# Sigmoid attention feeding a SiLU feed-forward: the x of one quad on two engines, one more gated pair of casts, all SBUF products on GpSimd, and a re-timed order

## The chip, the cores and the metric

The kernel runs on one core of a Trainium2 chip. Its time is the device time of one execution in microseconds, and a kernel is described by the median of several executions. The trace comes from one profiled execution; it records what each engine did and when: TensorE (PE, its weight loads PEld), VectorE (DVE), ScalarE (ACT), GpSimd (POOL), and the DMA queues issued from SyncE (SP), GpSimd and ScalarE.

## The reference

```python
# q, k, v: (8 batches, 12 heads, 448 positions, 64)
scores = (q @ k.T) / sqrt(64) - log(448)
attn = 1 / (1 + exp(-scores))          # a sigmoid, not a softmax
x = (attn @ v)                         # to 3584 tokens x 768
h = x @ w_in                           # w_in 768 x 2048
g = h * (1 / (1 + exp(-h)))
out = g @ w_out                        # w_out 2048 x 768, float32
```

## The kernel before

**Tiling.** Attention works on *quads*: four heads of one batch, so a batch has three quads and quad i belongs to batch i // 3. A quad's 448 keys are taken in seven *score steps* of 64 (`score_step`, line 172: four 64x64 matmuls into one pair of PSUM banks), each followed by a sigmoid on ScalarE (line 178) into `attnT`. When a quad's seven sigmoids are there, 28 matmuls multiply by v (`value_steps`, line 188), and `to_x` scales the sum into x, transposed, in half precision. `to_x` has three forms: two VectorE instructions when the sum lies in the two `ffp` banks (line 201), one VectorE instruction over both banks (line 206), or, with `shared`, one bank by VectorE (line 203) and the other by ScalarE (line 204).

PSUM has four pairs of banks: `att0`, `att1`, `att2` and the two `ffp` banks, which are called pair 3.

**Products by seven instead of eight.** From batch 1 on, both matrix products of the feed-forward are done blockwise with seven block products in place of eight, with sums of blocks as operands. `x_sums` (line 218) makes the sums of x, `w_in_sums` (317 to 319) and `w_in_last_sum` (323) those of w_in, `w_sum` (432, in two halves) those of w_out, `g_sums` (454 to 460) those of the gated hidden rows. `ff1(b, ...)` computes x times w_in for batch b: 14 groups of twelve L350 matmuls; ScalarE copies partial results to SBUF (381), VectorE combines them (385), ScalarE takes the sigmoid (369), and the product by the value follows. For six of eight results per batch that product reads SBUF only, and the table `GP` says for each whether GpSimd (371) or VectorE (373) does it; the other two read PSUM and are VectorE's. `ff2(n, rows, ...)` multiplies one or two blocks of 128 tokens by w_out (L473, eight matmuls per product); between its products VectorE copies (484), combines (487) and scales (506, 545) PSUM, and the stores go out from SP.

**The order.** Every engine runs its instructions in the order in which they are written, so the source decides the order; nothing is planned at run time.

- The opening is the list `INIT`: "s" is the next score step and its sigmoid, ("T", kind, quad, pair) transposes k (1) or q (0) of a quad with TensorE and copies it out with VectorE (158), ("V", quad, pair, r) a value step, "X" a `to_x`, "L" a load, "W" a quarter of w_in, "F" a number of steps of batch 0's first product `ff1_first`, "D" dummy matmuls that read a tile of zeros.
- `PROGRAM` then runs batch 0's first product (96 matmuls on line 282) and stops at the named steps for a "v", a visit of batch 1's attention (`visit`: up to two units, each a score step or the value steps of a quad with its x), or for one of the sums ("w", "l", "x", "y", "1", "2"; "f" writes a product that was put off, line 300). The last visit holds quad 5's value steps and its x.
- In stage b, from 1 to 7, `ff1(b)` runs, and then `ff2` on the blocks that are ready; `PHASES[b - 1]` says after how many L473 matmuls a visit of batch b+1's attention comes and how many units it takes.

**Loads of later quads.** k and q of quads 6 and on are loaded in float32 to `st32` by SP (`fetch`, 123), cast by GpSimd to `st16` (`cast`, 126), and transposed by a DMA from SP (`dma_transpose`, 140); v is loaded from GpSimd's queue (119). For each later quad j, `fetch(j)` is written after the visit with score step 0 of quad j-2, and `prepare(j)`, its two casts and two transposes, after the visit with score step 3 of that quad; for the first quad of the pair that a stage begins with, `prepare` stands at the start of the stage instead, behind two one-element memsets of `st16` on VectorE (738). A cast must wait for the memset of its tile, which runs in VectorE's order: that holds GpSimd's casts back until VectorE has come to that place.

Of the kernel before, what the change touches and what calls it, by code (L numbers as in the profile page):

```python
# [16 lines left out]
def kernel(  # L17
# [9 lines left out]
    nc = tc.nc  # L27

    B, H, S, D = q.shape
# [5 lines left out]
    NQ = H // 4  # L35
# [16 lines left out]
    def sb(name, shape, dtype=F16):  # L52
        return pool.tile(shape, dtype, tag=name, name=name)
# [15 lines left out]
    st16 = [sb(f"st16_{t}", [P, R, 2, D]) for t in range(2)]  # L69
# [126 lines left out]
    def to_x(i, pair, shared=False):  # L196
        b, n = divmod(i, NQ)
        x = xT[min(b, 1)].rearrange("p (j n) s -> p n j s", n=NQ)[:, n]
        if pair == 3:
            for j in range(2):  # L200
                nc.vector.tensor_scalar_mul(x[:, j], ffp[j][:, :S], SX)
        elif shared:
            nc.vector.tensor_scalar_mul(x[:, 0], att[pair][:, 0, :S], SX)
            nc.scalar.activation(x[:, 1], att[pair][:, 1, :S], AF.Copy, scale=SX)
        else:
            nc.vector.tensor_scalar_mul(x, att[pair][:, :, :S], SX)  # L206
# [4 lines left out]
    def x_sums(cs, lo=0, hi=4):  # L211
        x = xT[1]
        b11, b12 = x[:, cs, SH:], x[:, cs, :SH]
        ch = slice(cs.start + KC, cs.stop + KC)
        b21, b22 = x[:, ch, SH:], x[:, ch, :SH]
        t1, t2, t3, t4n = (xs[:, i, cs] for i in range(4))
        for o, p, q in ((t1, b12, b11), (t2, b22, t1), (t3, b22, b12), (t4n, b21, t2))[lo:hi]:
            nc.vector.tensor_sub(o, p, q)
# [4 lines left out]
    def flush():  # L223
        while later:
            later.pop(0)()

    def at(u, f):
        events.setdefault(u, []).append(f)
# [3 lines left out]
    def visit(us, n=3, hold=False):  # L232

        if not hold:
            flush()
        pairs = [p for p in used if p < n][: len(us)]
        for p in pairs:
            used.remove(p)
            used.append(p)
        for u in us:  # L240
            if u[0] == "a":
                pr = pairs.pop(0)
                value_steps(u[1], pr, range(R))
                to_x(u[1], pr)
                if u[1] >= 2 * NQ:
                    x_sums(slice(u[1] % NQ, u[1] % NQ + 1))
        for u in us:
            if u[0] == "s":
                pr = pairs.pop(0)
                score_step(u[1], u[2], pr)  # L250
                sigmoid(u[1], u[2], pr)
        for u in us:
            for f in events.pop(u, ()):
                f()
# [316 lines left out]
        load32(0, i)  # L571
        load16(2, i)

    def prepare(i):
        for t in (1, 0):
            cast(t, i)
            dma_transpose(t, i)
# [30 lines left out]
    def T(kind, i, pair):  # L608
# [3 lines left out]
            t_copy(kind, i, pair, half, dve)  # L612

    PROGRAM = (
        (8, "v", 0), (19, "v", 0), (32, "v", 0), (38, "v", 0), (43, "w", 1),
        (43, "v", 0), (50, "v", 0), (59, "w", 0), (59, "v", 0), (69, "v", 0),
        (71, "w", 3), (74, "v", 0), (86, "w", 2), (89, "v", 0), (94, "v", 0),
        (96, "l", 1), (96, "x", 0), (96, "x", 1), (96, "v", 0), (96, "x", 2),
        (96, "f", 0), (96, "l", 0), (96, "y", 2), (96, "y", 1), (96, "y", 0),
        (96, "1", 0), (96, "2", 0),  # L620
    )

    INIT = (
        ("L", 1, 3), ("D", 2), ("s",), ("s",), ("T", 1, 1, 2), ("s",), ("s",), ("s",),
        ("T", 0, 1, 3), ("L", 1, 4), ("s",), ("L", 0, 3), ("T", 1, 2, 2), ("L", 0, 4),
        ("s",), ("T", 0, 2, 3), ("s",), ("s",), ("L", 2, 1), ("L", 1, 5),
        ("T", 1, 3, 2), ("s",), ("V", 0, 2, 0), ("V", 0, 2, 1), ("V", 0, 2, 2),
        ("L", 2, 2), ("L", 0, 5), ("s",), ("W", 0), ("W", 1), ("V", 0, 2, 3),
        ("V", 0, 2, 4), ("T", 0, 3, 3), ("s",), ("V", 0, 2, 5), ("W", 2),
        ("V", 0, 2, 6), ("X", 0, 2), ("s",), ("T", 1, 4, 3), ("L", 2, 4), ("s",),  # L630
        ("s",), ("T", 0, 4, 2), ("L", 2, 5), ("V", 1, 3, 0), ("V", 1, 3, 1),
        ("L", 2, 3), ("s",), ("s",), ("T", 1, 5, 2), ("W", 3), ("s",), ("V", 1, 3, 2),
        ("T", 0, 5, 2), ("V", 1, 3, 3), ("s",), ("V", 1, 3, 4), ("V", 1, 3, 5), ("s",),
        ("s",), ("V", 2, 2, 0), ("V", 2, 2, 1), ("V", 2, 2, 2), ("V", 2, 2, 3),
        ("V", 1, 3, 6), ("s",), ("V", 2, 2, 4), ("V", 2, 2, 5), ("V", 2, 2, 6), ("s",),
        ("X", 1, 3), ("X", 2, 2, True), ("F", 4), ("F", 4),
    )

    us = units_of(1)
# [2 lines left out]
    for what, *a in INIT:  # L642
        if what == "s":
            u = scores[ns]
# [22 lines left out]
    for i in range(NQ + 1, B * NQ - 2):  # L667
        at(("s", i, 0), lambda j=i + 2: (gate(j) if j < 2 * NQ + 1 else None, fetch(j)))
        if i % NQ < NQ - 1:
            at(("s", i, 3), lambda j=i + 2: prepare(j))  # L670

# [14 lines left out]
    for n, kind, c in PROGRAM:  # L688
# [8 lines left out]


    PHASES = (
        ((19, 3), (33, 3), (46, 3), (58, 3), (67, 3), (82, 3), (89, 2), (97, 3), (107, 1)),  # L700
        ((19, 3), (33, 3), (47, 3), (53, 3), (62, 3), (76, 3), (85, 2), (91, 3), (107, 1)),
        ((19, 3), (33, 3), (48, 3), (54, 3), (63, 3), (77, 3), (85, 3), (91, 2), (99, 1)),
        ((17, 3), (32, 3), (46, 3), (53, 3), (62, 3), (76, 3), (83, 3), (92, 2), (97, 1)),
        ((14, 3), (23, 3), (37, 3), (40, 3), (47, 3), (58, 3), (62, 2), (67, 3), (75, 1)),
        ((19, 3), (32, 3), (44, 3), (50, 3), (60, 3), (75, 3), (83, 3), (91, 2), (99, 1)),
        (),
    )

    GP = (
        (1, 1, 1, 1, 1, 1), (1, 1, 1, 1, 1, 1), (1, 1, 1, 1, 0, 1), (1, 1, 1, 1, 1, 1),  # L710
        (1, 1, 1, 1, 1, 1), (1, 1, 1, 1, 1, 1), (0, 1, 1, 1, 1, 1),
    )

    ORD = (
# [15 lines left out]
    for b in range(1, B):  # L730
        parts = FF2[b - 1]
        late = (parts[0][0] + parts[0][1]) * P > b * S
        if parts[0][1] == 2 and not late:
            g_sums(parts[0][0], 4)
        if b + 1 < B:

            for t in range(2):
                nc.vector.memset(st16[t][:, 0, 0, 0:1], 0.0)  # L738
            prepare(b * NQ + NQ + 1)
        groups = ((1 - used[-1], 3), (2, used[-1])) if b == 1 else ((1, 3), (2, 0))  # L740
        used.sort()
        ff1(b, groups, GP[b - 1], ORD[b - 1])
        us = units_of(b + 1) if b + 1 < B else []

        def run():
            for i, (n, rows) in enumerate(parts):
                yield from ff2(n, rows, parts[i + 1][1] if i + 1 < len(parts) else 0, late and i == 0)

        it = run()
        done = 0  # L750
        nu = 0
        for target, m in PHASES[b - 1]:
            while done < target:
                next(it)
                done += 1
            visit(us[nu : nu + m])
            nu += m
        for _ in it:
            pass
# [30 lines left out]
```

## Time and profile before

| what | value |
|---|---|
| median of 7 runs | 374.09 us (373.25 to 375.67) |
| the profiled execution | 373.25 us |
| its span | 371.5 us |
| TensorE matmuls busy | 357.6 us (96%) |
| ScalarE busy | 255.3 us (69%) |
| VectorE busy | 229.4 us (62%) |
| GpSimd busy | 157.0 us (42%) |
| TensorE clock granted | full in all forty slices |

The span is what the trace covers; what lies around it makes up the rest of the execution's time. A line of the timeline gives the start, the time to the end of the last of its instructions, engine, line, operation, what is written and read with its size, the count, and in brackets the idle time of the engine ahead of it with what ended that. Matmuls overlap: one L473 matmul is drawn 0.33 us long while the next begins 0.163 us after it.

### The profile page before, as it was taken

How to read it: one execution, taken by the hardware profiler on the slowest of the kernel's cores; microseconds unless marked ns; L12 is line 12 of the kernel's file. 1: busy time of each engine (PE TensorE's matmuls, PEld its weight loads, DVE VectorE, ACT ScalarE, POOL GpSimd, SP SyncE). 2: the span in 40 equal slices, each digit the busy share in tenths (PEclk: the TensorE clock that was granted, in tenths of full speed). 3: DMA queues.
4: the chain of work that ended last, by engine and by line, in shares of the span. 5: the costliest groups of instructions: out<-in, count | busy, mean ns of one | idle time of the engine just before them, and what ended most of it. 6: DMA issues, size and time to landing. Idle time of an engine off the chain costs nothing. (4 is left out here: it accounts for less than half of the span.)

```text
span 371.5 us, 8711 instructions
## 1 busy us (share of the span) xinstructions
PE 357.6 (96%) x3596; PEld 239.1 (64%) x3596; DVE 229.4 (62%) x399; ACT 255.3 (69%) x290; POOL 157.0 (42%) x160
## 2 busy tenths in 40 slices
PE   8679999999999999999999999999999999999995
PEld 3344446964579655894549955598447965489663
DVE  2673689958765574586747656618367557437762
ACT  3999886777856798476874778567995779846200
POOL 8961430494305923169111782019630591004500
PEclk9999999999999999999999999999999999999999
DMA  8999999849897099563994539982699705130133
GB/s 143 191 171 205 232 224 180 155 104 165 130 237 161 6 172 211 159 150 50 193 211 118 123 52 204 205 188 48 85 180 220 164 11 116 38 86 2 42 87 86
DMA packets 64840, 51.14 MB, mean 138 GB/s; under 512 B 36896, under 2 KB 61728, under 8 KB 64800
## 3 DMA queue, kind: packets, MB, share of 16 engines
q1 hardware_dynamic: 48544, 35.24, 44.6%
q0 software_dynamic: 15328, 14.32, 25.9%
q10 hardware_dynamic: 928, 1.02, 0.8%
q8 instruction: 28, 0.46, 0.5%
q14 instruction: 12, 0.10, 0.1%
HBM read 45.61 MB, written 11.01 MB: 152 GB/s over the span
## 5 line engine op out<-in xcount | busy, mean ns | idle before, releaser
L178 ACT ACTIVATE attnT<-att,bias_s 128x896 f16<-128x896 f32 x168 | 157.3, 1008 | 28.9 <-PE att L172 28.4
L371 POOL TENSOR_TENSOR gT<-attnT,gT 128x896 f16<-128x896 f32 x40 | 75.2, 1908 | 56.2 <-ACT gT L369 56.1
L126 POOL CAST st<-st 128x896 f16<-128x896 f32 x36 | 33.8, 960 | 123.1 <-DVE st L738 54.4
L350 PEld LDWEIGHTS <-w_in_sb 128*128 128x128 f16 x672 | 64.4, 98 | 1.8 <-issue 0.9
L350 PE MATMUL att<-xT,w_in_sb 128*128 128x224 f16 x588 | 61.2, 259 | 0.4 <-DVE xT L206 0.4
L473 PEld LDWEIGHTS <-gT 128*128 128x128 f16 x416 | 39.1, 98 | 29.9 <-issue 6.5
L381 ACT COPY attnT<-att 128x896 f32<-128x896 f32 x35 | 31.7, 905 | 38.5 <-PE att L350 38.3
L473 PEld LDWEIGHTS <-gs 128*128 128x128 f16 x384 | 34.8, 98 | 32.6 <-issue 12.3
L369 ACT ACTIVATE gT<-attnT 128x896 f16<-128x896 f32 x42 | 39.9, 951 | 17.6 <-DVE attnT L385 16.3
L473 PE MATMUL ffp<-w_out_sb,gT 128*128 128x384 f16 x288 | 51.5, 326 | 0.0
L350 PEld LDWEIGHTS <-sw 128*128 128x128 f16 x504 | 48.3, 98 | 0.0
L172 PE MATMUL att<-qkT,qkT 64*64 64x448 f16 x588 | 41.9, 358 | 4.2 <-ACT attnT L178 3.4
L206 DVE TENSOR_SCALAR xT<-att 128x896 f16<-128x896 f32 x22 | 24.0, 1091 | 27.3 <-PE att L188 24.1
L385 DVE TENSOR_TENSOR attnT<-att,attnT 128x896 f32<-128x896 f32 x28 | 30.5, 1090 | 15.1 <-PE att L350 14.2
L473 PE MATMUL ffp<-wt,gs 128*128 128x384 f16 x192 | 35.9, 327 | 0.5 <-DVE snap L484 0.5
L473 PE MATMUL ffp<-w_out_sb,gs 128*128 128x384 f16 x192 | 36.1, 327 | 0.0
L350 PE MATMUL att<-xT,sw 128*128 128x224 f16 x336 | 35.0, 259 | 0.0
L484 DVE TENSOR_SCALAR snap<-ffp 128x384 f32<-128x384 f32 x40 | 22.1, 553 | 19.4 <-PE ffp L473 19.3
L188 PE MATMUL att<-attnT,v 64*64 64x448 f16 x588 | 32.5, 352 | 1.3 <-DVE wt L158 0.9
L487 DVE SCALAR_TENSOR_TENSOR osb<-ffp,snap 128x384 f32<-128x384 f32 x40 | 22.1, 553 | 16.5 <-PE ffp L473 16.2
L172 PEld LDWEIGHTS <-qkT 64*64 64x64 f16 x588 | 16.6, 105 | 24.5 <-issue 19.0
L385 DVE TENSOR_TENSOR attnT<-ffp,attnT 128x448 f32<-128x448 f32 x28 | 16.1, 616 | 25.6 <-PE ffp L350 14.4
(73 smaller groups left out, 344.2 us busy)
## 6 DMA issues: line engine op xcount, KB each, us to landing
out_dram<-osb SPq DMA_DIRECT2D x48, 192.0 KB, 3.4
st<-in_k_dram SPq DMA_DIRECT2D x36, 224.0 KB, 4.6
st<-in_q_dram SPq DMA_DIRECT2D x36, 224.0 KB, 5.3
v<-in_v_dram POOLq DMA_DIRECT2D x44, 112.0 KB, 4.4
w_in_sb<-in_moe_w_in_dram POOLq DMA_DIRECT2D x4, 768.0 KB, 12.2
w_out_sb<-in_moe_w_out_dram POOLq DMA_DIRECT2D x4, 768.0 KB, 18.6
sw<-in_k_dram POOLq DMA_DIRECT2D x8, 112.0 KB, 4.3
sw<-in_q_dram POOLq DMA_DIRECT2D x8, 112.0 KB, 4.3
```

Of the source, the lines that this page charges most:

```text
L126: nc.gpsimd.tensor_copy(st16[kind].rearrange("p r e d -> p e r d"), st32[kind].rearrange("p e (r d) -> p e r d", r=R),)
L172: nc.tensor.matmul(att[pair][cj, e, :S], kT[re, r, cj], qT[re, :, cj], start=True, stop=True)
L178: nc.scalar.activation(attnT[:, s0 : s0 + 2, :], att[pair][:, :, :S], AF.Sigmoid, bias=bias_s, scale=QKSCALE)
L188: nc.tensor.matmul(bank(pair, j)[e * HP : (e + 1) * HP, :S], vt[rj, e, r, :], attnT[rj, s0 + e, :], start=(r == 0), stop=(r == R - 1),)
L206: nc.vector.tensor_scalar_mul(x, att[pair][:, :, :S], SX)
L350: nc.tensor.matmul(o, a[:, c, (4 * s + f) * P : (4 * s + f + 1) * P], xb[:, c], start=first and c == 0 and f % 2 == 0, stop=c == KC - 1, s ...
L369: nc.scalar.activation(oo, ap, AF.Sigmoid, bias=0.0, scale=ISX)
L371: nc.gpsimd.tensor_mul(oo, ap, oo)
L381: nc.scalar.copy(as2(h[:, i, c], ap), ap)
L385: nc.vector.tensor_add(as2(h[:, i, c], ap), ap, as2(h[:, i, c], ap))
L473: nc.tensor.matmul(bank, a[:, fc], w[:, fc], start=first and fc == 0, stop=fc == KH - 1, skip_group_check=True,)
L484: nc.vector.tensor_scalar_mul(snap[i], bank, ISX)
```

## The change

Five things change.

- `visit` passes `hold` on to `to_x`. Only the last visit of `PROGRAM` is called with `hold`, so the x of quad 5, batch 1's last, is made by lines 203 and 204 instead of 206. In `PROGRAM`, the two x sums of index 1 are now written after that visit, not ahead of it.
- `prepare` takes over the two memsets that stood at the head of each stage, and quad 8 (`2 * NQ + 2`) gets them too. In VectorE's order they come right after the third sum of w_out (line 432, written to `w_out_sb`), ahead of the next copy on line 484.
- `GP` is all ones: two products by the value that VectorE did, one in stage b=3 and one in stage b=7, are GpSimd's.
- `INIT` loses its two dummy matmuls, and some of its entries change places.
- In `PROGRAM` and `PHASES` some visits, and one w_in sum, come at other steps.

```diff
-                to_x(u[1], pr)
+                to_x(u[1], pr, hold)
...
-    def prepare(i):
+    def prepare(i, behind=False):
+        if behind:
+            for t in range(2):
+                nc.vector.memset(st16[t][:, 0, 0, 0:1], 0.0)
         for t in (1, 0):
             cast(t, i)
             dma_transpose(t, i)
...
     PROGRAM = (
-        (8, "v", 0), (19, "v", 0), (32, "v", 0), (38, "v", 0), (43, "w", 1),
-        (43, "v", 0), (50, "v", 0), (59, "w", 0), (59, "v", 0), (69, "v", 0),
+        (8, "v", 0), (16, "v", 0), (32, "v", 0), (38, "v", 0), (43, "w", 1),
+        (43, "v", 0), (51, "v", 0), (53, "w", 0), (58, "v", 0), (69, "v", 0),
         (71, "w", 3), (74, "v", 0), (86, "w", 2), (89, "v", 0), (94, "v", 0),
-        (96, "l", 1), (96, "x", 0), (96, "x", 1), (96, "v", 0), (96, "x", 2),
+        (96, "l", 1), (96, "x", 0), (96, "v", 0), (96, "x", 1), (96, "x", 2),
...
     INIT = (
-        ("L", 1, 3), ("D", 2), ("s",), ("s",), ("T", 1, 1, 2), ("s",), ("s",), ("s",),
-        ("T", 0, 1, 3), ("L", 1, 4), ("s",), ("L", 0, 3), ("T", 1, 2, 2), ("L", 0, 4),
-        ("s",), ("T", 0, 2, 3), ("s",), ("s",), ("L", 2, 1), ("L", 1, 5),
-        ("T", 1, 3, 2), ("s",), ("V", 0, 2, 0), ("V", 0, 2, 1), ("V", 0, 2, 2),
-        ("L", 2, 2), ("L", 0, 5), ("s",), ("W", 0), ("W", 1), ("V", 0, 2, 3),
-        ("V", 0, 2, 4), ("T", 0, 3, 3), ("s",), ("V", 0, 2, 5), ("W", 2),
-        ("V", 0, 2, 6), ("X", 0, 2), ("s",), ("T", 1, 4, 3), ("L", 2, 4), ("s",),
-        ("s",), ("T", 0, 4, 2), ("L", 2, 5), ("V", 1, 3, 0), ("V", 1, 3, 1),
-        ("L", 2, 3), ("s",), ("s",), ("T", 1, 5, 2), ("W", 3), ("s",), ("V", 1, 3, 2),
+        ("L", 1, 3), ("s",), ("s",), ("T", 1, 1, 2), ("s",), ("s",), ("s",),
+        ("T", 0, 1, 3), ("L", 0, 3), ("L", 1, 4), ("s",), ("T", 1, 2, 2), ("s",),
+        ("L", 0, 4), ("s",), ("T", 0, 2, 3), ("s",), ("L", 2, 1), ("L", 1, 5),
+        ("T", 1, 3, 2), ("s",), ("V", 0, 2, 0), ("V", 0, 2, 1), ("s",), ("L", 2, 2),
+        ("V", 0, 2, 2), ("L", 0, 5), ("W", 0), ("W", 1), ("V", 0, 2, 3), ("V", 0, 2, 4),
+        ("T", 0, 3, 3), ("V", 0, 2, 5), ("s",), ("V", 0, 2, 6), ("X", 0, 2),
+        ("T", 1, 4, 3), ("s",), ("s",), ("W", 2), ("T", 0, 4, 2), ("s",), ("L", 2, 5),
+        ("V", 1, 3, 0), ("V", 1, 3, 1), ("L", 2, 4), ("L", 2, 3), ("s",), ("s",),
+        ("W", 3), ("T", 1, 5, 2), ("s",), ("V", 1, 3, 2), ("T", 0, 5, 2),
...
-        ("X", 1, 3), ("X", 2, 2, True), ("F", 4), ("F", 4),
+        ("X", 1, 3), ("F", 4), ("X", 2, 2, True), ("F", 4),
...
-            at(("s", i, 3), lambda j=i + 2: prepare(j))
+            at(("s", i, 3), lambda j=i + 2: prepare(j, j == 2 * NQ + 2))
...
     PHASES (first to sixth row; only what differs)
-     b=1: (89, 2), (97, 3)      b=2: (85, 2), (91, 3)      b=3: (99, 1)
+     b=1: (90, 3), (97, 2)      b=2: (89, 2), (95, 3)      b=3: (98, 1)
-     b=5: (62, 2)               b=6: (60, 3)
+     b=5: (63, 2)               b=6: (59, 3)
...
     GP
-     b=3: (1, 1, 1, 1, 0, 1)    b=7: (0, 1, 1, 1, 1, 1)
+     b=3: (1, 1, 1, 1, 1, 1)    b=7: (1, 1, 1, 1, 1, 1)
...
         if b + 1 < B:
-            for t in range(2):
-                nc.vector.memset(st16[t][:, 0, 0, 0:1], 0.0)
-            prepare(b * NQ + NQ + 1)
+            prepare(b * NQ + NQ + 1, True)
```

## The prediction

> **What bounds the kernel now.** I read the busy shares, then TensorE's rows in order of time for idle spots, then what the other engines did at each.
>
> ```profile
> PE 357.6 (96%) x3596; PEld 239.1 (64%) x3596; DVE 229.4 (62%) x399; ACT 255.3 (69%) x290; POOL 157.0 (42%) x160
> PEclk9999999999999999999999999999999999999999
> ```
>
> TensorE is busy for 96% of 371.5 us, at full clock in every slice: the order of its work sets the end, and an edit is worth only what it takes from or adds to TensorE's idle spots. Before 30 us there are many short ones, behind ScalarE's sigmoids and VectorE's copies. After it they are few, and two groups come from VectorE.
>
> First group, stage b=1:
>
> ```profile
> 83.06 0.96 DVE L432 TENSOR_TENSOR w_out_sb<-w_out_sb 128x1536 f16<-128x1536 f16 x1
> 83.94 3.10 DVE L432 TENSOR_TENSOR w_out_sb<-w_out_sb 128x1536 f16<-128x1536 f16 x1
> 84.39 1.83 POOL L126 CAST st<-st 128x896 f16<-128x896 f32 x2
> 87.56 1.46 PE L473 MATMUL ffp<-wt,gT 128*128 128x384 f16 x8 [0.82 <-DVE snap L484]
> ```
>
> The second half of the third w_out sum takes 3.10 us where the first took 0.96: quad 8's two casts run beside it. The copy L484 is queued behind it (86.96), and TensorE waits for that copy. The row says 0.82; one L473 matmul is drawn 0.33 long but the next follows after 0.163 (23.41 us for 144), so the real loss is 0.82 + 0.16 = 0.98.
>
> Second group, stage b=3:
>
> ```profile
> 161.24 8.29 POOL L371 TENSOR_TENSOR gT<-attnT,gT 128x896 f16<-128x896 f32 x4 [3.60 <-ACT gT L369]
> 165.02 2.76 DVE L373 TENSOR_TENSOR gT<-attnT,gT 128x896 f16<-128x896 f32 x1
> 170.30 0.65 PE L473 MATMUL ffp<-wt,gs 128*128 128x384 f16 x3 [0.22 <-DVE snap L484]
> 171.75 0.38 PE L172 MATMUL att<-qkT,qkT 64*64 64x448 f16 x4 [0.30 <-DVE gT L373]
> 183.46 0.93 POOL L126 CAST st<-st 128x896 f16<-128x896 f32 x1 [7.61 <-DMA st<-in_k_dram]
> 183.56 1.38 DVE L460 TENSOR_TENSOR gs<-gT,gs 128x1024 f16<-128x1024 f16 x1
> 185.46 0.97 PE L473 MATMUL ffp<-wt,gs 128*128 128x384 f16 x5 [0.28 <-DVE snap L484]
> ```
>
> Here VectorE does one product by the value from SBUF (2.76 us beside GpSimd's products; in stage b=7 the same form, alone, took 1.08), so the L385, L484 and L373 behind it are late, and 15 us later a cast stretches L460 from its usual 0.68 to 1.38. The three losses, with 0.16 each as above: 0.38 + 0.46 + 0.44 = 1.28.
>
> **The change, part by part.**
>
> *Casts of quad 8 gated.* Two more memsets (59 ns each in the groups by form) stand behind the third sum. Both halves then take 0.95, as the other six L432 did: it ends at 84.88 instead of 87.04. L484 then goes when its product is done (84.7) or right after the memsets, 84.95 to 85.5; TensorE reaches its user at 86.58. Saved: 0.98. Late next: the casts, held to about 85.05 (in other stages the cast follows the memset by 0.15) and done by 86.9, 0.7 later than now. Behind them on GpSimd stand v of quad 9 and its casts; on SP quad 8's transposes, quad 9's loads and a store; the quad 9 tiles are needed a stage later. The next L432 pair starts near 87.35, 0.45 after the casts; if they met, VectorE would lose up to 2.15 (3.10 - 0.95), with a later L206 and up to 1 us of TensorE.
>
> A rule speaks against this saving. The Trainium skill (SBUF — State Buffer, Who interferes with whom) says that a VectorE instruction with two SBUF inputs and a GpSimd one that reads SBUF lock each other out, and that whoever issued first holds the lock. The sum began 0.45 before the casts, so the rule would have the casts wait, the sum last 0.95, and this edit bring 0. The row shows the reverse: the casts took their usual 0.93, the sum 3.10. I take the row.
>
> *Products all on GpSimd.* In b=3 GpSimd does six: 6 x 1.853 (b=1: 11.12 for six) from 161.24 ends at 172.36 instead of 171.73. VectorE loses the 2.76, so L385 starts when its product is ready (166.36), L484 at 168.8, the last L373 at 169.3, in the places which the same rows have in b=1, where TensorE waits for none. Saved 0.38 + 0.46. The later cast meets L460 no more: GpSimd ends 0.63 later while VectorE is 0.84 earlier, so L460 is over about half a microsecond before the cast lands. Saved 0.44. Queued behind GpSimd's longer list: v and casts of quad 14, then SP's transposes (landed 180.98, needed near 186) and quad 15's loads, not needed in this stage. In b=7 the product took 1.08 with TensorE never waiting: worth 0. Six of 1.884 from 337.9 end at 349.2, still before the sum L454 that reads them (349.79): cost 0, and at most 0.5 if GpSimd is slower.
>
> *x of the last quad by two engines.*
>
> ```profile
> 59.82 1.09 DVE L206 TENSOR_SCALAR xT<-att 128x896 f16<-128x896 f32 x1
> 60.97 0.54 PE L350 MATMUL att<-xT,w_in_sb 128*128 128x224 f16 x4 [0.39 <-DVE xT L206]
> 61.45 1.08 DVE L300 TENSOR_TENSOR gT<-att,gT 128x896 f16<-128x896 f32 x1
> 62.59 1.31 PE L350 MATMUL att<-xT,w_in_sb 128*128 128x224 f16 x12
> ```
>
> The half on VectorE takes 0.61 (L203, seen once), ScalarE's 0.55 (L204), and TensorE's first wait of 0.5 goes. But two x sums now stand behind it, so L300 starts at 61.4 as before. TensorE's third product writes the bank that L300 reads: it began at 62.59, 0.06 after L300's end. The wait moves there. Saved: 0.02, and no more than 0.3.
>
> *Opening.*
>
> ```profile
> 7.60 0.55 DVE L158 CAST qkT<-att 128x384 f16<-128x384 f32 x1
> 7.73 0.59 PE L87 MATMUL ffp<-warm 128*128 128x512 f16 x2 [0.37 <-DVE qkT L158]
> 8.26 0.57 PE L172 MATMUL att<-qkT,qkT 64*64 64x448 f16 x8
> 8.69 9.09 ACT L178 ACTIVATE attnT<-att,bias_s 128x896 f16<-128x896 f32 x10 [0.98 <-PE att L172]
> ```
>
> Without the two dummies the first score waits only for the copies that end at 7.71, so the sigmoids start 0.47 earlier, at 8.2. From there I follow the written order with the trace's own distances: sigmoid 0.44 after its score; a score on the same bank 1.06 after the earlier sigmoid's start; sigmoids 0.91 apart; a transpose group 0.58 of TensorE, its copies on VectorE from 0.46 after its start for 1.15; 0.19 per value step. The first value step waits for the copies before it, 16.9 (now 17.28). The 11th sigmoid starts at 17.7 (18.28). Three value steps and a transpose group then stand before the 12th score: 19.34 (19.49). A transpose group now precedes the 13th score and waits for copies until 19.9: 20.66 (20.41). The 17th score 23.56 (23.24), the group behind it and its copies, 19th sigmoid 26.9 (26.62). The first feed-forward matmul then starts at 30.25 instead of 29.97: **+0.28**. The loads land in time for this (the last transposed ones 22.9, the first w_in piece 29.1). Ends: -0.47 if the early start is kept, +0.75 if the first score doesn't come earlier.
>
> *Visits.* At step 16 instead of 19 the second score needs a sigmoid that has not ended: +0.09 after what the next waits give back. At 51 and 58 instead of 50 and 59, the second score of the latter stands 0.24 before its bank is free (now it is free to the hundredth): +0.24. In b=1, 2, 3 and 6 the moved visits keep their banks free by my count: 0. In b=5, 62 to 63, ScalarE is dense: the x that the next visit's bank waits for (L206, 276.58 to 277.67, freed 0.02 late now) comes 0.16 later: +0.16.
>
> Sum: -0.98 - 1.28 - 0.02 + 0.28 + 0.09 + 0.24 + 0.16 = -1.5. The profiled execution took 373.25 for a span of 371.5, and was the fastest of seven; it would become 371.7. From the median of 374.09 I predict **372.6**.
>
> **Rivals.**
> 1. *The opening keeps its head start*: -0.47 instead of +0.28 and no new visit stalls, sum -2.6, 371.5. For it: ScalarE bounds the opening. Against: the places counted above.
> 2. *Collisions only move*: the held casts meet the next L432, and L460's stays (1 us and 0.44 back): sum -0.1, 374.0. For it: casts follow DMA landings, which shift by tenths. Against: gaps of about 0.5 on both.
> 3. *Slower: quad 8's transposes come too late.* Now q's is issued at 86.85, lands at 92.95, and its first score runs at 95.91. Held casts put it at about 88.1, landing 94.2 if it again takes 6.1 us, while the score moves to 95.5: slack 1.3. Beyond that TensorE waits one for one. The sum is zero when it takes 8.9 us, and 10 us give +1.1, 375.2 and more. For it: transposes took up to 15.2 us to land while weights were being loaded. Against: the median is 4.4, and no weights load then.
>
> **How the numbers follow.** 0.3%, about what a measurement can tell, is 1.1 us: faster is below 372.97, slower above 375.21. The forecast has 0.55 (its own range 371.8 to 373.3; 0.45 faster, 0.10 same), rival 1 0.15, rival 2 0.20, rival 3 0.10. So faster 0.60, same 0.30, slower 0.10. The range leaves out rival 3 and the ends of the others: 371.3 to 374.4.
>
> **What would show it.** Right: third sum's second half near 0.95 with no wait before the L473 after it; six L371 in b=3 and no L373 from attnT; L460 at 0.7; first sigmoid near 8.2, first L282 near 30.2; the third L350 product still starting with L300's end. Wrong: an L172 of quad 8 waiting for a DMA near 95; a stretched L432 after 87; L282 starting much before or after 30.

## The result, and the profile after

The changed kernel's median is **371.60 us** (371.02 to 373.12, 24 executions); the kernel before, run beside it, had 373.70 (372.10 to 377.18, 61). The ratio is 0.9943, 95% interval 0.9931 to 0.9955: 2.1 us less, where 1.5 were forecast (1.1 from the 373.70 of this comparison to the 372.6 on record). The profiled execution took 371.34 us with a span of 369.5, so the two profiled executions differ by 1.9. The 371.60 lies 0.2 below the range that the prediction gave to its own forecast (371.8 to 373.3) and inside the whole one (371.3 to 374.4).

The page of the changed kernel, its busy shares:

```profile
PE 357.1 (97%) x3594; PEld 238.8 (65%) x3594; DVE 222.3 (60%) x399; ACT 256.0 (69%) x291; POOL 159.6 (43%) x162
PEclk9999999999999999999999999999999999999999
```

TensorE does the same work (two matmuls fewer) in a shorter span; VectorE lost 7 us of busy time, GpSimd gained 2.6. Where the 1.9 us went is read from TensorE's start times, since its work is in nearly the same order in both. The column "lead" is the start in the changed kernel minus the start in the kernel before; minus means earlier.

| mark on TensorE | lead, us | gained or lost since the mark above | predicted |
|---|---|---|---|
| first L282, end of the opening | -0.14 | -0.14 | +0.28 |
| 25th L282, behind the visit at 16 | 0.00 | +0.14 | +0.09 |
| 61st L282, behind the visit at 58 | +0.27 | +0.27 | +0.24 |
| 85th L282 | +0.11 | -0.16 | 0 |
| third product of b=1 | +0.07 | -0.04 | -0.02 |
| first L350 of b=2 | -0.90 | -0.97 | -0.98 |
| first L350 of b=4 | -2.22 | -1.32 | -1.28 |
| first L350 of b=6 | -2.06 | +0.16 | +0.16 |
| first L350 of b=7 | -2.06 | 0 | 0 |
| last matmul | -2.06 | 0 | 0 |

Behind TensorE's last matmul the changed kernel's span goes on for 0.11 us longer than the other's, so the spans differ by 1.9.

Stage b=1 of the changed kernel, lines in order of time (start, length, engine, line, operation):

```profile
82.02 1.88 POOL L371 TENSOR_TENSOR gT<-attnT,gT 128x896 f16<-128x896 f32 x1
83.14 1.59 DVE L432 TENSOR_TENSOR w_out_sb<-w_out_sb 128x1536 f16<-128x1536 f16 x1
84.64 0.94 DVE L432 TENSOR_TENSOR w_out_sb<-w_out_sb 128x1536 f16<-128x1536 f16 x1
85.53 0.55 DVE L484 TENSOR_SCALAR snap<-ffp 128x384 f32<-128x384 f32 x1
85.54 0.07 DVE L578 MEMSET st<- 128x1 f16 x2
85.76 1.81 POOL L126 CAST st<-st 128x896 f16<-128x896 f32 x2 [0.65 <-issue]
86.66 1.46 PE L473 MATMUL ffp<-wt,gT 128*128 128x384 f16 x8
87.33 1.04 DVE L432 TENSOR_TENSOR wt<-w_out_sb,wt 128x1536 f16<-128x1536 f16 x1
```

The gate works: the casts come behind the memsets, the second half takes 0.94, and the L473 row has no wait. The first half takes 1.59, though, and no cast is near it: what is beside it is GpSimd's last product. Two things differ from the account ahead of the prediction. On VectorE the memsets come behind the copy L484 (85.54 against 85.53), not ahead of it; so the casts start at 85.76 instead of about 85.05. And they end at 87.57, not 86.9, when the next w_out sum (87.33) has already begun.

Stage b=3 of the changed kernel:

```profile
160.34 11.13 POOL L371 TENSOR_TENSOR gT<-attnT,gT 128x896 f16<-128x896 f32 x6 [3.60 <-ACT gT L369]
169.01 0.65 PE L473 MATMUL ffp<-wt,gs 128*128 128x384 f16 x3
169.59 0.76 PE L172 MATMUL att<-qkT,qkT 64*64 64x448 f16 x12
181.78 0.68 DVE L460 TENSOR_TENSOR gs<-gT,gs 128x1024 f16<-128x1024 f16 x1
182.39 0.93 POOL L126 CAST st<-st 128x896 f16<-128x896 f32 x1 [6.79 <-DMA st<-in_k_dram]
183.24 0.98 PE L473 MATMUL ffp<-wt,gs 128*128 128x384 f16 x5
```

Six products on GpSimd, no wait in the three TensorE rows (each had one before), and L460 is nearly over (0.07 left) when the cast starts.

The seam into stage b=1 of the changed kernel:

```profile
59.93 0.62 DVE L203 TENSOR_SCALAR xT<-att 128x448 f16<-128x448 f32 x1 [0.70 <-PE att L188]
61.53 1.08 DVE L300 TENSOR_TENSOR gT<-att,gT 128x896 f16<-128x896 f32 x1
62.66 1.31 PE L350 MATMUL att<-xT,w_in_sb 128*128 128x224 f16 x12 [0.26 <-DVE gT L300]
```

The first wait is gone and the third product waits for L300 instead.

The opening of the changed kernel:

```profile
7.61 0.76 PE L172 MATMUL att<-qkT,qkT 64*64 64x448 f16 x8 [0.54 <-DVE qkT L158]
8.04 9.09 ACT L178 ACTIVATE attnT<-att,bias_s 128x896 f16<-128x896 f32 x10 [0.62 <-PE att L172]
29.84 1.69 PE L282 MATMUL ffp<-xT,w_in_sb 128*128 128x448 f16 x8
```

The first sigmoid starts at 8.04 (forecast 8.2), the first L282 at 29.84 (forecast 30.25).

### The profile page after: what moved, and what is told of

The parts are those of the page before. It is cut to its first block, busy times and chain, and to the rows that moved or that the text cites. A ratio compares the mean times of both kernels' runs of the same rounds, so it can differ in the third digit from the quotient of the medians.

```text
span 369.5 us, 8711 instructions
## 1 busy us (share of the span) xinstructions
PE 357.1 (97%) x3594; PEld 238.8 (65%) x3594; DVE 222.3 (60%) x399; ACT 256.0 (69%) x291; POOL 159.6 (43%) x162
## 4 chain that ended last, share of the span: by engine, by line
PE 90%; ACT 5%; DVE 2%; issue 1%; DMA 1%; POOL 0%; ACTq 0%; DVEq 0%
PE ffp L473 35%; PE att L350 24%; PE att L172 9%; PE att L188 9%; PE ffp L350 6%; ACT attnT L178 4%; PE att L282 2%; PE ffp L282 2%; PE ffp L87 1%; DMA sw<-in_q_dram 1%; DVE wt L158 1%; PE att L148 1%; PE ffp L148 0%; DVE gT L300 0%; DVE gT L373 0%
## 5 line engine op out<-in xcount | busy, mean ns | idle before, releaser
L371 POOL TENSOR_TENSOR gT<-attnT,gT 128x896 f16<-128x896 f32 x42 | 77.9, 1885 | 54.3 <-ACT gT L369 54.3
L350 PEld LDWEIGHTS <-w_in_sb 128*128 128x128 f16 x672 | 64.4, 98 | 1.6 <-issue 0.8
L350 PE MATMUL att<-xT,w_in_sb 128*128 128x224 f16 x588 | 61.2, 259 | 0.3 <-DVE gT L300 0.3
L473 PEld LDWEIGHTS <-gT 128*128 128x128 f16 x416 | 39.1, 98 | 28.7 <-issue 5.3
L473 PEld LDWEIGHTS <-gs 128*128 128x128 f16 x384 | 34.9, 98 | 31.9 <-issue 11.5
L473 PE MATMUL ffp<-w_out_sb,gT 128*128 128x384 f16 x288 | 51.5, 326 | 0.0
L350 PEld LDWEIGHTS <-sw 128*128 128x128 f16 x504 | 48.3, 98 | 0.1
L385 DVE TENSOR_TENSOR attnT<-att,attnT 128x896 f32<-128x896 f32 x28 | 30.5, 1091 | 17.2 <-PE att L350 16.2
L206 DVE TENSOR_SCALAR xT<-att 128x896 f16<-128x896 f32 x21 | 22.9, 1090 | 26.5 <-PE att L188 26.5
L473 PE MATMUL ffp<-w_out_sb,gs 128*128 128x384 f16 x192 | 36.3, 327 | 0.0
L473 PE MATMUL ffp<-wt,gs 128*128 128x384 f16 x192 | 35.8, 327 | 0.0
L484 DVE TENSOR_SCALAR snap<-ffp 128x384 f32<-128x384 f32 x40 | 22.2, 554 | 21.3 <-PE ffp L473 21.3
L350 PE MATMUL att<-xT,sw 128*128 128x224 f16 x336 | 35.0, 259 | 0.0
L172 PEld LDWEIGHTS <-qkT 64*64 64x64 f16 x588 | 16.9, 105 | 24.4 <-issue 18.3
L385 DVE TENSOR_TENSOR attnT<-ffp,attnT 128x448 f32<-128x448 f32 x28 | 16.1, 616 | 25.7 <-PE ffp L350 14.4
```

The source lines that it names most:

```text
L172: nc.tensor.matmul(att[pair][cj, e, :S], kT[re, r, cj], qT[re, :, cj], start=True, stop=True)
L350: nc.tensor.matmul(o, a[:, c, (4 * s + f) * P : (4 * s + f + 1) * P], xb[:, c], start=first and c == 0 and f % 2 == 0, stop=c == KC - 1, s ...
L371: nc.gpsimd.tensor_mul(oo, ap, oo)
L385: nc.vector.tensor_add(as2(h[:, i, c], ap), ap, as2(h[:, i, c], ap))
L473: nc.tensor.matmul(bank, a[:, fc], w[:, fc], start=first and fc == 0, stop=fc == KH - 1, skip_group_check=True,)
L484: nc.vector.tensor_scalar_mul(snap[i], bank, ISX)
```

## The experiments

The traces account for 1.9 us, and by the table 0.97 of it is the gate and 1.32 the products. Do the medians say so too, and what is the 0.14 of the opening? In the diffs below, "+" and "-" are against the kernel named.

**The four parts, one at a time.** Each is the kernel before with one part of the change.

```diff
 gate_only   +  at(("s", i, 3), lambda j=i + 2: prepare(j, j == 2 * NQ + 2))
 gp_only     +  GP = all ones
 x_only      +  to_x(u[1], pr, hold)     (with its place of the x sum in PROGRAM)
 order_only  +  INIT, PHASES and the visits in PROGRAM of the changed kernel
```

> The kernel before with quad 8's casts gated and nothing else. Theory (TensorE's idle spots decide, and the casts stretch the third w_out sum): both halves of that sum near 0.95 to 1.6, no wait of TensorE for the copy on line 484 near 87, stage b=2 starting 0.98 us earlier, ratio 0.9974. Rival (the sum is slow for another reason, the v loads from GpSimd or its own operands): the second half stays near 3.1 us and the ratio is 1.000. Rival (quad 8's transposed q comes too late): a wait of TensorE near 95, ratio above 0.998.

> The kernel before with the product table all ones and nothing else. Theory: 0.84 us won where stage b=3's second product begins, 0.44 more if the later cast no longer meets the sum on line 460; 1.28 in all, ratio 0.9966, nothing in stage b=7. Rival (GpSimd's longer list makes its later casts late): the stretch of line 460 stays and only 0.84 us is won, ratio 0.9978; or TensorE waits for a product of GpSimd in b=7 near 349, ratio 0.998 or more.

> The kernel before with quad 5's x on two engines and the two x sums behind it, nothing else. Theory: TensorE's wait of about 0.5 us at the third chunk of the first L350 product goes, and comes back at the third product, which starts with the end of line 300's product on VectorE (62.6): 0.0 us, ratio 1.000. Rival (the wait was the loss): third product at 62.1, ratio 0.9987.

> The kernel before with the new order in INIT, PROGRAM and PHASES, nothing else of the change (quad 5's x whole on VectorE, its sums in the old place). From the profile after: first feed-forward matmul 0.1 to 0.2 us earlier, 0.14 lost at step 16, 0.27 at step 58 of which 0.16 comes back, 0.16 lost in b=5: 0.2 to 0.3 us slower, ratio 1.0007. By the sum of the prediction (opening +0.28, visits +0.33, b=5 +0.16): 0.8 us slower, ratio 1.002.

The kernel before had 373.94 beside these (372.73 to 376.61).

| kernel | median, us | range | ratio (95%) | by medians | predicted |
|---|---|---|---|---|---|
| gate_only | 372.25 | 371.86 to 372.86 | 0.9946 (0.9931 to 0.9962) | -1.69 | -0.98 |
| gp_only | 373.24 | 371.79 to 375.77 | 0.9983 (0.9960 to 1.0006) | -0.70 | -1.28 |
| x_only | 374.16 | 373.15 to 376.89 | 1.0007 (0.9986 to 1.0028) | +0.22 | -0.02 |
| order_only | 373.76 | 373.04 to 374.38 | 0.9991 (0.9979 to 1.0004) | -0.18 | +0.77 (0.28 + 0.09 + 0.24 + 0.16) |

They add up to -2.35, near the -2.1 of the whole. The gate's interval, -2.6 to -1.4, leaves out the 0.98 that one trace showed; the order's, -0.79 to +0.15, leaves out the +0.77 forecast, and by a little the ratio of 1.0007 (+0.26) expected from the profile after. The products' interval, -1.5 to +0.2, holds both the 1.28 forecast and 0. The executions of gate_only lie within 1.0 us, those of gp_only within 4.0 (those of order_only, ungated too, within 1.3). The profiled execution of gp_only shows one of the long ones. Its third w_out sum (VectorE), GpSimd beside it, and TensorE behind it:

```profile
82.89 1.90 POOL L371 TENSOR_TENSOR gT<-attnT,gT 128x896 f16<-128x896 f32 x1
83.12 2.48 DVE L432 TENSOR_TENSOR w_out_sb<-w_out_sb 128x1536 f16<-128x1536 f16 x1
85.53 3.08 DVE L432 TENSOR_TENSOR w_out_sb<-w_out_sb 128x1536 f16<-128x1536 f16 x1
85.95 1.84 POOL L126 CAST st<-st 128x896 f16<-128x896 f32 x2
88.53 0.55 DVE L484 TENSOR_SCALAR snap<-ffp 128x384 f32<-128x384 f32 x1
89.13 2.49 PE L473 MATMUL ffp<-wt,gT 128*128 128x384 f16 x8 [2.32 <-DVE snap L484]
```

Both halves are stretched here, by 1.53 and 2.13, and TensorE waits 2.48 (2.32 and the usual 0.16). The busy times by stretch of the same execution (its length, busy us of PE, PEld, DVE, ACT, POOL with counts, then the granted clock, the DMA share and GB/s):

```profile
89.40:92.80 3.40, 3.40 (x18) 1.43 (x19) 2.07 (x3) 0.00 (x0) 0.00 (x0) 0.50 1.03 120
92.80:96.00 3.20, 3.20 (x45) 1.60 (x41) 1.81 (x5) 1.71 (x2) 0.00 (x0) 1.00 1.12 221
```

Behind the long wait TensorE runs at half clock, for 3.41 us. Stage b=1 lost 4.64 us in this execution. So the size of this stall changes from execution to execution.

The clock is not what makes the gate worth more than 0.98. For each execution the mean granted clock is known too; one stretch of 3.41 us at half clock brings it down to 0.994 or 0.995 (gp_only, x_only, after_final), two to 0.991 (nodummy_only). Of the executions with 0.997 or more, the kernel before has a median of 373.71 (24 of 53) and gate_only of 372.14 (8 of 16): 1.57 apart.

**The gate taken out of the changed kernel, and the casts on another engine.** The second of these is the kernel before, ungated.

```diff
 after_ungated (changed kernel)
-            at(("s", i, 3), lambda j=i + 2: prepare(j, j == 2 * NQ + 2))
+            at(("s", i, 3), lambda j=i + 2: prepare(j))
 act_casts (kernel before)
-        nc.gpsimd.tensor_copy(
+        (nc.scalar.copy if i == 2 * NQ + 2 else nc.gpsimd.tensor_copy)(
```

> The changed kernel with quad 8's two casts ungated again (the two memsets behind the third w_out sum are left out). Theory (the casts beside the third sum cost 1 us as a rule, and more in a part of the executions, when the sum's first half is stretched too and TensorE waits long): the second half of L432 takes about 3.1 us again, stage b=1 loses at least 0.97 us in the trace, the median rises by about 1.5 to 1.9 us over the changed kernel, to near 373.3, with a wide spread (over 2.5 us between its fastest and slowest). What is left against the kernel before is b=3's gain. Rival (only what the traces showed counts, 0.97): the median rises by 1.0, to 372.6, and the spread stays near 1.5 us. Rival (gating was not needed once the other edits were made): same as the changed kernel.

> The kernel before with quad 8's two casts on ScalarE instead of GpSimd, ungated, at the same place. Theory (GpSimd and VectorE hinder each other when both read SBUF): the second half of L432 takes about 0.95 us although two casts of the same tiles run near it, L484 is not late, and the 0.98 us of stage b=1 is saved less what two more instructions of about 1 us on ScalarE cost its own chain (0 to 1 us): 373 to 374 us. Rival (any engine that writes those tiles or reads SBUF at that moment stretches the sum): the second half of L432 still takes 2 us or more while the casts run beside it, and nothing is gained: 374 us or more.

The kernel before had 373.95 beside these two and the next two. after_ungated: 373.32 (372.20 to 373.83), ratio 0.9974 (0.9958 to 0.9990). Against the changed kernel's 371.60 the gate is worth 1.7 us, as it was alone, and 1.70 again among executions with a clock of 0.997 or more (373.24, 16 of 22, against 371.54, 21 of 25 with the profiled one). The two were not timed in one comparison: by their ratios to the kernel before, it is 1.2 us (0.4 to 1.9). That the gate was no longer needed is ruled out; that only the 0.98 of the two traces counts is put out by gate_only's interval, not by this run. In its profile both halves are stretched:

```profile
82.77 1.89 POOL L371 TENSOR_TENSOR gT<-attnT,gT 128x896 f16<-128x896 f32 x1
83.36 2.10 DVE L432 TENSOR_TENSOR w_out_sb<-w_out_sb 128x1536 f16<-128x1536 f16 x1
85.39 3.09 DVE L432 TENSOR_TENSOR w_out_sb<-w_out_sb 128x1536 f16<-128x1536 f16 x1
89.00 1.30 PE L473 MATMUL ffp<-wt,gT 128*128 128x384 f16 x7 [1.95 <-DVE snap L484]
```

The expected wide spread did not come (1.6 us), and TensorE kept its full clock in this one.

act_casts: 372.72 (372.19 to 375.18), ratio 0.9974 (0.9959 to 0.9989), 0.3 below what was expected. With the casts on ScalarE, the second half of the sum takes 0.95 and TensorE no longer waits for L484:

```profile
85.72 1.78 ACT L126 CAST st<-st 128x896 f16<-128x896 f32 x2
86.54 1.46 PE L473 MATMUL ffp<-wt,gT 128*128 128x384 f16 x8
87.39 4.80 ACT L178 ACTIVATE attnT<-att,bias_s 128x896 f16<-128x896 f32 x5
```

The casts take 1.78 of ScalarE's time and make the sigmoids behind them late (0.48 lost at the visit that follows; with the 1.23 gained by the medians that makes about 1.7, the gate's worth once more). What this run can't tell is whether ScalarE could also stretch a sum: its queue let the casts start only at 85.72, when the third sum was all but over (85.78). It shows that the stall leaves with GpSimd's casts, not more.

**The wait moved by the shared x, and the moved visits.** Both start from the changed kernel.

```diff
 after_split
-        (96, "l", 1), (96, "x", 0), (96, "v", 0), (96, "x", 1), (96, "x", 2),
-        (96, "f", 0), (96, "l", 0), (96, "y", 2), (96, "y", 1), (96, "y", 0),
+        (96, "l", 1), (96, "x", 0), (96, "v", 0), (96, "t", 1), (96, "t", 2),
+        (96, "f", 0), (96, "u", 1), (96, "u", 2), (96, "l", 0), ...
+        acts["t", c] = lambda c=c: x_sums(slice(c, c + 1), 0, 1)
+        acts["u", c] = lambda c=c: x_sums(slice(c, c + 1), 1, 2)
 after_best, on top
-        (8, "v", 0), (16, "v", 0), ...  (51, "v", 0), (53, "w", 0), (58, "v", 0)
+        (8, "v", 0), (19, "v", 0), ...  (50, "v", 0), (59, "w", 0), (59, "v", 0)
-        ... (58, 3), (63, 2), (67, 3), (75, 1)),
+        ... (58, 3), (62, 2), (67, 3), (75, 1)),
```

> The changed kernel, with the two x sums that stand between the last x of batch 1 and L300 (the sum that frees the bank of TensorE's third product) split: only the part that the second product needs stays ahead of L300, the other part goes behind it. Theory (the saving of the shared x was eaten because VectorE is the next bound: the third product started with L300's end, 62.66 us in the changed kernel): L300 ends about 0.5 us earlier, the third product starts near 62.15, stage b=1 starts 0.5 us earlier, and the time falls by 0.4 to 0.5, to 371.1. Rival (the wait moves once more, to the fourth product or to the parts of the sums that went behind): the third product starts earlier but the first score of b=1 doesn't: 371.6, no change.

> As the run before it (split x sums), and with the feed-forward visits of the first stage and stage b=5's one moved place put back to the places of the kernel before (19, 50, 59, 59 instead of 16, 51, 53, 58; 62 instead of 63). Theory (by the comparison of the two traces these moves lost 0.41 and gave 0.16 back in the first stage, and lost 0.16 in b=5): another 0.3 to 0.4 below the run before it, 370.7 to 370.8. Rival (the second part of the visits' loss is given back by what follows, as 0.16 of it was): equal to the run before it within 0.15.

after_split: 371.23 (370.84 to 372.12, six executions), ratio 0.9930 (0.9904 to 0.9956). The third product starts at 62.17 with no wait, 0.5 earlier, just as expected. But in this execution all of it is lost again by the first L350 of b=2, in a place that neither theory named (the median is 0.37 below the changed kernel's, too little to tell from 0 or from 0.5 by six executions):

```profile
82.61 1.90 POOL L371 TENSOR_TENSOR gT<-attnT,gT 128x896 f16<-128x896 f32 x1
82.64 2.67 DVE L432 TENSOR_TENSOR w_out_sb<-w_out_sb 128x1536 f16<-128x1536 f16 x1
86.12 0.55 DVE L484 TENSOR_SCALAR snap<-ffp 128x384 f32<-128x384 f32 x1
86.72 1.46 PE L473 MATMUL ffp<-wt,gT 128*128 128x384 f16 x8 [0.40 <-DVE snap L484]
```

TensorE and VectorE came 0.5 earlier to the third sum, GpSimd 0.6 later than in the changed kernel (its list starts behind quad 7's q cast, which waits for that quad's load), so the last product now covers 1.86 us of the first half. The sum ends 0.81 after the product, almost as if it had just begun (0.95 alone).

after_best: 371.27 (370.36 to 371.91, six executions), ratio 0.9928 (0.9904 to 0.9952). In its trace the visits give back 0.40 by the 61st L282 less the 0.16 that came back anyway, b=5 gives 0.16, and b=1 loses nothing (first half 1.92, just short enough): 0.9 with the seam. Its opening was 0.50 later than the changed kernel's, so 0.4 is left, and its profiled time is 370.91. Its median is no different from after_split's, and above the 370.7 to 370.8 expected.

**The product out of the sum's way.** Quad 7's q cast goes on GpSimd behind the first L371 product of b=1 instead of before it; alone on the changed kernel (after_lateq), and on after_best (after_final).

```diff
-            prepare(b * NQ + NQ + 1, True)
+            prepare(b * NQ + NQ + 1, True, (1,) if b == 1 else (1, 0))
+        if b == 1:
+            behind_first.append(lambda: prepare(2 * NQ + 1, True, (0,)))
...
                     nc.gpsimd.tensor_mul(oo, ap, oo)
+                    if behind_first:
+                        behind_first.pop()()
```

> The changed kernel with the split x sums, the visits of the first stage and of b=5 at their old places, and quad 7's q cast moved on GpSimd from before the six L371 products to behind the first of them. Theory (the third w_out sum stands still while the last L371 product runs, and that product ends late because the list starts only after the q cast, which waits for its load): L371 ends about 0.9 us earlier against the first L350 than in the changed kernel, before the sum starts or within 0.2 of it, the first half of L432 takes 0.95 to 1.15, and b=1 loses nothing of the 0.5 us that the split sums gain, in each execution: 370.6 to 370.9. Rival (quad 7's later q makes a score late, or the list is held by its sigmoids instead): the first half of L432 still takes 1.4 us or more, or a wait appears before a score of quad 7; 371.2 or more.

> The changed kernel with that one move of quad 7's q cast alone. Theory: the first half of L432 falls from 1.59 us to 0.95 to 1.15, but L484 was not late in the changed kernel, so the profiled time stays (371.3) and the median gains only what rare executions lost: 371.3 to 371.6. Rival (the sum's stretch does not come from the L371 product): first half unchanged at 1.4 us or more.

The kernel before had 373.75 beside these. In both the stretch is gone; after_final (its lines are numbered 2 to 4 higher: L373 is the product of line 371, L436 the sum of line 432):

```profile
73.94 9.26 POOL L373 TENSOR_TENSOR gT<-attnT,gT 128x896 f16<-128x896 f32 x5
83.33 1.82 DVE L436 TENSOR_TENSOR w_out_sb<-w_out_sb 128x1536 f16<-128x1536 f16 x2
```

The list ends at 83.20, before the sum starts, and the two halves together take 1.82. Stage b=1 loses nothing in either. By the medians this is small: after_final 371.11 (370.66 to 371.39, five executions), ratio 0.9930 (0.9918 to 0.9942), 0.2 above the range expected; after_lateq 371.95 (371.47 to 372.83, six), ratio 0.9959 (0.9945 to 0.9973), which is 0.35 above the range expected. Two of its six executions had a clock of 0.994 or less (372.62, 372.83); the other four have a median of 371.63. Its profiled execution (371.68) was late by 0.35 at the first L282 and kept that lag to the end, so what it lost to the changed kernel's is the opening's. after_final's profiled execution was late by 0.96 there and still ended only 0.06 behind the changed kernel's. The ledger of its later stages (visits, seam, b=1, b=5) is 0.90 better; the median shows some 0.5, with the openings' spread in it.

**The opening.** Kernel before with the new INIT alone, and with the two dummies out and nothing else.

```diff
 init_only      INIT of the changed kernel
 nodummy_only
-        ("L", 1, 3), ("D", 2), ("s",), ("s",), ...
+        ("L", 1, 3), ("s",), ("s",), ...
```

> The kernel before with the changed opening's order alone (without the two dummy products), the visits left. The first L282 starts at 29.97 us in the kernel before and 29.84 in the changed one. The prediction's reckoning: 30.25. Theory now (its copies were reckoned too late): 29.8 to 30.1, unless the clock falls to half in the opening, which adds about 1 us.

> The kernel before without the two dummy products of the opening, its order left. Theory (the order keeps the head start of 0.47 us that the first score gains): the first L282 near 29.5. Rival (the copies and the loads set the start of the later steps, and the head start is used up on the way, whatever the order): 29.9 to 30.0, as in the kernel before.

One execution each: 372.76 and 373.88. init_only:

```profile
7.76 0.75 PE L172 MATMUL att<-qkT,qkT 64*64 64x448 f16 x8 [0.54 <-DVE qkT L158]
16.78 0.57 PE L188 MATMUL att<-attnT,v 64*64 64x448 f16 x8 [0.86 <-DMA sw<-in_q_dram]
29.99 0.74 PE L282 MATMUL ffp<-xT,w_in_sb 128*128 128x448 f16 x3
```

This opening starts where the prediction had it start (first sigmoid near 8.2) and reaches the first L282 at 29.99, not 30.25: the reckoning was 0.26 too long, for the same start. nodummy_only settles nothing: TensorE fell to half clock from 10.9 to 17.7 us in it, as the clock's row shows,

```profile
PEclk9699999999999999999999999999999999999999
```

and its first L282 came at 31.20. Half clock in the opening is nothing that the missing dummies do by themselves: x_only, which has them, had 3.41 us of it (first L282 at 31.00), after_final 3.41 us (30.80), and the seven other profiled kernels without them none. Leaving these three out, the first L282 started at 29.84, 29.85, 29.99, 30.06, 30.09, 30.18 and 30.34 with the new opening and at 29.94, 29.97, 30.03 and 30.36 with the old one. So the two openings end alike, but not for want of a difference. From the first score to the first L282 the new one took 22.22 to 22.24 us in all seven, the old one 21.72 in three and 21.85 in gp_only: the new order loses 0.5 us. It begins earlier by about as much, its first score at 7.61 to 8.10 against 8.18 to 8.64. The spread of the openings at full clock is that of their starts.

The clock tells one thing more. Of the executions with the old opening 87 of 173 had a mean clock below 0.997, of those with the new one 22 of 92 (init_only and nodummy_only, one execution each, not counted); among gated kernels alone it is 8 of 16 against 11 of 48. So a stretch at half clock seems rarer with the new opening. Where in the execution it fell is known for the profiled ones alone, and the one execution of nodummy_only can't tell whether the order or the missing dummies do it. It may be why order_only's median lies 0.2 under the kernel before though its trace is 0.4 longer; that is not shown.

## Why the prediction was right, and where it was not

The gate and the products are the gain, as forecast, and both act where the prediction said. That the sum came so near is in part luck: by the medians of the single parts the gate gave 0.7 us more than its term and the order took 0.95 less, while the products gave 0.6 less.

**Gated casts: right in the cause, too small by 0.7 us.** In the two traces the step gained 0.97 where 0.98 was forecast, but by medians 1.7 alone, and 1.2 to 1.7 when taken out of the changed kernel. The term was too small because it took the 0.98 of one execution for every execution. What stage b=1 lost beyond the length it has when nothing is late (29.62 us from its last L350 to the first of b=2):

| kernels | loss in b=1, one profiled execution each |
|---|---|
| ungated: nodummy_only, init_only, before, order_only, x_only, after_ungated, gp_only | 0.37, 0.51, 0.97, 1.23, 1.37, 2.11, 4.64 |
| gated: changed, gate_only, after_best, after_lateq, after_final, after_split | 0, 0, 0, 0, 0, 0.56 |

The means are 1.60 and 0.09, a difference of 1.5, which is near the 1.7 of the medians. Two things make the spread, besides the clock, which fell in one of the seven (of gp_only's 4.64, 2.48 are the wait). One is that the sum has a second neighbour, GpSimd's last product, and the first half's 0.96 in the profile of before was that execution's luck (the product ended 0.14 after the sum's start). In each of the ten executions in which the product began first and ended after the sum's start, the first half ended 0.81 to 0.82 after the product: 1.21 long in order_only, 1.59 in the changed kernel, 2.67 in after_split. The prediction's "both halves then take 0.95" was wrong for that reason; it cost nothing in the changed kernel, as L484 was still done (86.08) about half a microsecond before TensorE came for it (86.66). The other is which of the two begins first. In init_only the sum's first half did, by 0.11; then the product was late, and the second half, behind it, took 2.63:

```profile
83.46 0.96 DVE L432 TENSOR_TENSOR w_out_sb<-w_out_sb 128x1536 f16<-128x1536 f16 x1
83.57 2.60 POOL L371 TENSOR_TENSOR gT<-attnT,gT 128x896 f16<-128x896 f32 x1
84.35 2.63 DVE L432 TENSOR_TENSOR w_out_sb<-w_out_sb 128x1536 f16<-128x1536 f16 x1
86.91 0.55 DVE L484 TENSOR_SCALAR snap<-ffp 128x384 f32<-128x384 f32 x1
87.35 1.83 POOL L126 CAST st<-st 128x896 f16<-128x896 f32 x2
87.50 1.46 PE L473 MATMUL ffp<-wt,gT 128*128 128x384 f16 x8 [0.36 <-DVE snap L484]
```

Its casts came behind the copy, so no gate on them would have saved its 0.51.

The place of the memsets was read wrongly as well: they stand behind L484, and the casts run 0.7 later than reckoned. That cost nothing here.

The prediction also weighed the Trainium skill's rule (SBUF — State Buffer, Who interferes with whom: whoever issued first holds the lock) against the row, and took the row. For the gain that was the right choice (the casts took 0.96 each in that row, 0.93 when gated). Two other meetings obey the rule in both directions, the cast beside L460 (next paragraph) and the product beside the first half: where it began first the sum waited, and in init_only, where the sum began 0.11 earlier, the sum took 0.96 and the product 2.60. The casts beside the second half do not: in five executions the second half began 0.4 before the first cast and still ended 0.82 after the last one. Nor does nodummy_only, where both halves (1.77, 1.68) and both casts (1.45, 1.65) were long. Whether GpSimd had the lock before the cast's recorded start, the rows don't say, and nothing was tried for it.

**Products all on GpSimd: right in the trace.** 1.32 against 1.28 (0.38 + 0.46 + 0.44). Stage b=3 took 44.32 to 44.34 us in the seven profiled executions with this edit, and 0.88 to 1.32 more in the seven without it: the 0.84 of the late L385, L484 and L373 is in each of them. The third term, the cast beside L460, is again a matter of the execution: of the seven kernels that leave the product on VectorE, two lost it (before and nodummy_only, where the cast began 0.10 and 0.14 before L460), in the other five L460 began first, by 0.09 to 0.38, and the cast waited. In order_only:

```profile
184.17 0.68 DVE L460 TENSOR_TENSOR gs<-gT,gs 128x1024 f16<-128x1024 f16 x1
184.26 1.39 POOL L126 CAST st<-st 128x896 f16<-128x896 f32 x1 [7.79 <-DMA st<-in_k_dram]
```

Here the 0.46 of waiting fell on a cast that nobody was waiting for. So the 0.44 was gained against one trace of before and is not gained against most. The median of gp_only, 0.7 with an interval of -0.2 to 1.5, fits 0.9 and can't tell it from 1.28.

**Shared x: right.** -0.04 at the seam, with the third product waiting for L300 as forecast; by the median it can't be told from 0. That the wait would move was shown by removing the next cause: in after_split the third product starts 0.5 earlier.

**Opening: the step that failed, by its size.** +0.28 was forecast, -0.14 seen. The mechanism was right: the first sigmoid comes earlier (0.49 in init_only) and the new order loses that on the way. But the loss from the first score to the first L282 was put at 0.75 and is 0.51 (22.23 against 21.72). Init_only, which has the forecast's own start, shows where: the first value step, forecast for 16.9 behind VectorE's copies, ran at 16.78 (they ended at 16.73, though the row names a load), and the sigmoids forecast for 17.7, 19.34, 20.66 and 26.9 started at 17.59, 19.18, 20.43 and 26.63. So the reckoning was 0.12 late at the first value step and 0.27 late behind the transpose groups, and never more. The rest of the difference, 0.15, is the start itself: the first score came at 7.61 in the changed kernel's trace and at 7.76 in init_only's. The right reading was: no difference, with a spread of 0.5 and, now and then, 1 us more.

**Visits, b=5: right.** 0.14 and 0.27 lost against 0.09 and 0.24; what was missed is that the 85th L282 had 0.16 of it back. b=5 lost 0.16 as forecast. The same losses, within 0.01, stand in all five profiled kernels with these places.

**The rivals.** The slower one (quad 8's q too late) is refuted: it landed at 93.63 and its first score ran at 95.01, a slack of 1.4 where 1.3 was reckoned. The collisions that "only move" did move into the next sum, if little: in the changed kernel its first half began 0.24 before the casts' end and took 1.04, in after_best 1.38, in after_split 1.72, each ending 0.81 after the casts. TensorE lost nothing by it (after_split's 0.56 is its wait for L484). The first rival came nearest to the time, 371.5, but by the wrong way: it let the opening keep 0.47 and the visits cost nothing; the opening gave 0.14, the visits cost 0.25 in all, and the missing gain is the gate's.

## What to carry to other kernels

Price a collision between two engines over several executions: its size depends on which of two loosely coupled engines is first by tenths, and one execution shows one size. A wait that comes and goes is worth removing for more than one trace says. When you move an engine's start earlier, list everything that runs on its neighbour at the new time; in after_split the half microsecond saved at the seam was lost again twenty microseconds later, beside a product that a late load had moved the other way.

## What the hardware showed unexpectedly

- A w_out sum makes almost no progress while a GpSimd product that began before it runs: of the 0.95 us that it takes alone, 0.81 to 0.82 were left after the product's end in ten executions, whatever the overlap was (0.14 to 1.86 us). Two back-to-back casts held a sum off together: in init_only one that began at 88.03, beside the first of two casts (87.35 to 89.19), took 1.98 and ended 0.82 after the second.
- A TensorE wait of 2.48 us was followed by 3.41 us at half clock (gp_only, 89.4 to 92.8), one of 2.11 in after_ungated was not. The length is that of the window which the Trainium skill gives (TensorE: Matmul & The Clock Gate, What's actually happening), but TensorE had not stood idle for a whole one: from 86.0 to 89.4 it was busy for 1.08 of 3.40 us. Half clock also came in three of fourteen openings, for 3.41 or 6.83 us. In the 3.41 us ahead of it TensorE was busy for 1.97, 2.17 and 2.03 us; in gate_only, which kept its full clock, for 1.79 and 2.03 in two such stretches (4.4 to 7.8, 14.6 to 18.0). What decides it stays open.
